# A sink-attention mixer on one core: weight sums by VectorE alone in buffers of their own, made late in two chunks, with the block order of the third batch and the pair order of the last turned

## Chip, cores and metric

The kernel runs on one core of a Trainium2 chip. The metric is device time in microseconds (us); the figure shown is the median of three runs. One further execution was profiled, and all rows below come from it.

## What is computed

```
q, k, v: 4 batches x 8 heads x 768 x 64; n_sink = 4, window = 128
scores = q k^T / 8, kept where column < n_sink or 0 <= row - column < window
x   = softmax(scores) v, heads side by side: 4 x 768 x 512
u   = x + (x^T U V)^T                       U 768 x 32, V 32 x 768
out = u + max(u w_ch1, 0) w_ch2             w_ch1 512 x 2048, w_ch2 2048 x 512
```

## The kernel before

The feed-forward part (FFN) is most of the work. Its 2048 hidden units are 16 **blocks** f of 128; a batch's 768 rows are two **chunks** c of 384. For each batch b, chunk and block, TensorE makes the hidden values (`l1`, L1251 to L1253: 12 matmuls, each number as a high and a low part), ScalarE or VectorE the relu's high part `hh` (L1259, L1260), VectorE its low part `hl` (L1262), and TensorE adds the block's share of the output (`l2`, L1272: 9 matmuls). A block with its weights is one tile `w` of 1 MB. Blocks 0 and 8 stay in two fixed tiles (`w_174`, `w_175`); the other 14 share four tiles (`w_176` to `w_179`) and come back from DRAM copies (`wd`) whenever their turn comes (L522).

Batches are numbered 0 to 3. Batch 0 goes over the blocks in groups while the weights are narrowed to the two-part form on VectorE and ScalarE (L108 to L116, L514). Batches 1 and 2 run one chunk after the other, (1,0), (1,1), (2,0), (2,1), with 16 blocks each: blocks 15 to 0 where c is 0, 0 to 15 where c is 1. So the blocks at a turn are still in their tiles. Beside the FFN of batch b the kernel does the attention of batch b+1 and then its *mixing* (the U V term: L936 to L1030, tiles `xT`, `xhl`, `t`). In the text a block is counted through the kernel: 0 to 31 in batch 0, 32 to 47 in (1,0), 48 to 63 in (1,1), 64 to 79 in (2,0), 80 to 95 in (2,1).

The last batch (`ffn_last`) takes blocks in pairs j = 0 to 7 and makes the hidden values with seven products instead of eight (L1139). For that it needs sums and differences of each pair's weights. `sums` makes them while both blocks lie in their tiles during batches 1 and 2: two adds of high and low part (`w`, 512 wide), four sums or differences 256 wide, then a copy to the high part and a subtraction for the low part, both 1024 wide; 16 stores of 512 KB write them to `sd`. `SUMS` says in which chunk a pair's sums are made: pairs 0 to 3 in (1,1), 7 to 4 in (2,0). The adds go through `tt`, which leaves it to the planner whether VectorE or GpSimd does them; the tiles `a` and `t` come from `raw`, a ring of four buffers `big` that also carries the outputs (L1298) and their residual rows `xd`.

All steps are recorded in a `Plan`. It is run forward and backward over a table of costs, then with shaken priorities from three `SEEDS`; the best order found is written out, engine by engine. Each engine works its list strictly in order, and nearly all DMAs are in one list, SyncE's. 30 idle matmuls fill gaps (L1376).

Of the kernel before, what the change touches and what calls it, by code (L numbers as in the profile page):

```python
# [15 lines left out]
U16 = mybir.dt.uint16  # L16
# [23 lines left out]
NPF = NF // 2  # L40
SUMS = {(1, 1): (0, 1, 2, 3), (2, 0): (7, 6, 5, 4)}
NEG = 8.0e9
# [6 lines left out]
TURNS = 4  # L49
SEEDS = (300012, 300023, 300026,)  # L50
SLACK = 0.0344
# [5 lines left out]
NSTREAM = 4  # L57
NBIG = 4
NNR = 6
NHH = 2  # L60
# [188 lines left out]
class Plan:  # L249
# [116 lines left out]
    def forward(self):  # L366
        avail = dict.fromkeys(self.SYNC, 0.0)
        ready = {e: [] for e in avail}
        dma = port = 0.0

# [33 lines left out]
        while done < len(self.steps):  # L404
# [22 lines left out]
            if e == "SP" and s.lat < 0.0:  # L427
                end = -s.lat
                dma = max(dma, end - 1.3)
            elif e == "SP":  # L430
                dma = max(dma, t + s.dur + 0.65) + s.lat
                end = dma + 1.3
# [47 lines left out]
class Fast:  # L480
# [44 lines left out]
    def narrow(self, src, n, prio, dst=()):  # L525

        raw, A, S_ = self.raw(), self.nr(), self.nr()
        if len(self.early) > 0:
            self.early.pop(0)
            self.plan.add("SP", 0.0, lambda: None, w=(raw,), lat=-EARLY[NBIG - 1 - len(self.early)], prio=-1e6)  # L530
        else:
            self.put(raw, lambda: (raw().bitcast(U16)[:, 1:4 * n + 1], src), P * n * 8, prio - 8.0)
        x = self.bank() if dst else None
        box = {"raw": raw, "a": A, "s": S_}
        cost = (0.069 + n * 0.52e-3, 0.069 + n * 0.26e-3, 0.069 + n * 0.26e-3, dve(n), 0.069 + n * 0.26e-3, dve(n), dve(n))
        steps = narrow_steps(self.nc, raw, n, lambda: A()[:, :n], lambda: S_()[:, :n], x and (lambda: x()[:, :n]))
# [12 lines left out]
        return raw, lambda: f32(raw())[:, 1:2 * n + 1:2]
# [492 lines left out]
    def seven(self, b, t0):  # L1042
# [38 lines left out]
        self.u[b, 0] = out  # L1081

    def sums(self, j, ws, prio):

        a, t = self.raw(), self.raw()
        fa, ft = (lambda x=x: f32(x()[:, :2 * DM]) for x in (a, t))
        for i, w in enumerate(ws):
            self.tt(DM, lambda i=i: fa()[:, i * DM:(i + 1) * DM], lambda w=w: f32(w()[:, 0]), lambda w=w: f32(w()[:, 1]), ALU.add,
                    r=((w, 0), (w, 1)), w=((a, i),), prio=prio)
# [3 lines left out]
        for i, o, x, y, op, r in ((0, s1, a21, a22, ALU.add, []), (1, s2, s1, a11, ALU.subtract, [(t, 0)]),  # L1093
                                  (2, s3, a11, a21, ALU.subtract, []), (3, s4, a12, s2, ALU.subtract, [(t, 1)])):
            self.tt(K2, o, x, y, op, r=[(a, 0), (a, 1)] + r, w=((t, i),), prio=prio)
        hi, lo = (lambda x=x: x()[:, :2 * DM].bitcast(F32R) for x in (a, t))
        self.copy(2 * DM, hi, ft, r=(t,), w=(a,), prio=prio)
        self.tt(2 * DM, lo, ft, lambda: f32(hi()), ALU.subtract, r=(a,), w=(t,), prio=prio)
        sd = self.sd[j]
# [4 lines left out]
    def ffn_last(self, b, prio):  # L1104

        nc, add = self.nc, self.plan.add
        late = self.recent[:]
        order = late[2:] + [None] + late[:2] + [None]
        fixed = [self.w[f] for f in range(NF) if f not in STREAMED]
        slots = [(NRES + self.held[f][0], self.held[f][1], f) if f is not None else (i // 3, fixed[i // 3], None) for i, f in enumerate(order)]  # L1110

# [14 lines left out]
        def l1(n):  # L1126
            j = NPF - 1 - n
            w1, w2, wt = unit(2 * j, self.wd[2 * j]), unit(2 * j + 1, self.wd[2 * j + 1]), unit(None, self.sd[j])
# [51 lines left out]
            p1 = product(x, r12, w1, half(w1, 0), 0, True, self.line)  # L1180
            self.line = (p1,)
            product(y, r2, w1, half(w1, 1), 1, True)
            snap(sa, ta, 0)
# [148 lines left out]
    def run(self):  # L1332
# [7 lines left out]
        self.ust, self.vst = one([P, NB, P], F32R, "ust"), one([P, S], F32R, "vst")  # L1340
        self.t = ring(2, [P, DM], F32R, "t")
        self.wtiles, self.banks, self.bigs, self.accs, tiles = [], [], list(self.early), [], []
        bigs = Ring(NBIG, None)
# [42 lines left out]
        for b in range(B):  # L1386
# [4 lines left out]
            else:  # L1391
# [3 lines left out]
                for c in range(NCHUNK):  # L1395
                    self.ffn(b, c, ORDER[::-1] if c == 0 else ORDER, 70.0 + 80.0 * (NCHUNK * b + c), False)
            if b + 1 < B:
# [165 lines left out]
def sink_attention_mixer(ctx, tc, q, k, v, vs, limits, U, V, w1, w2, out):  # L1563
# [5 lines left out]
    with tc.tile_pool(name="work", bufs=1) as work, tc.tile_pool(name="idle", bufs=1, space=PSUM) as idle, \  # L1569
# [16 lines left out]
        for src, n in ((U, NB * RANK), (V[0], VC), (V[1], VC), (w1[ORDER[0]], DM))[:NBIG]:  # L1586
            early.append(pre.tile([P, RAW], I32, name=f"big{len(early)}"))
            nc.sync.dma_start(early[-1].bitcast(U16)[:, 1:4 * n + 1], src)
        tri = sp.tile([P, 2, P], F32, name="tri")
# [69 lines left out]
```

## Time and profile before

| | |
|---|---|
| median of 3 runs | 747.08 us (745.52 to 747.18) |
| the profiled execution's own time | 747.41 us |
| its span, first to last instruction | 745.7 us |
| TensorE busy | 725.6 us (97%), 4032 matmuls |
| VectorE, ScalarE, GpSimd busy | 494.8, 369.6, 219.8 us |

TensorE's share of 97% counts pipelined matmuls from issue to end. What it waits for is seen better in PEld, its weight loads: one that waits is listed with what it waited for. The granted TensorE clock was full speed in all slices of the page.

### The profile page before, as it was taken

The page shows a single profiled execution, that of the slowest core. Times are in us where ns is not written, and L with a number is a line of the kernel's source. Part 1 is how long each engine was busy: PE and PEld are TensorE (multiplying, and loading weights), DVE is VectorE, ACT ScalarE, POOL GpSimd, SP SyncE. Part 2 cuts the span into 40 slices and gives each one's busy share as a digit, 9 for nine tenths or more (in the row PEclk, how much of TensorE's full clock was granted, in tenths as well). Part 3 has the DMA queues.
Part 4 walks back from the last instruction along what each step waited for, and adds up shares of the span by engine and source line. Part 5 has one row for each costly group of instructions (what it writes and reads, how often), then busy time and mean ns, then how long its engine had stood idle before and what let it go on. Part 6 is the DMA issues. An engine that isn't in the chain of part 4 may idle for free.

```text
span 745.7 us, 11814 instructions
## 1 busy us (share of the span) xinstructions
PE 725.6 (97%) x4032; PEld 626.5 (84%) x4032; DVE 494.8 (66%) x1209; ACT 369.6 (50%) x1029; POOL 219.8 (29%) x337
## 2 busy tenths in 40 slices
PE   8989999999998999999999999999999999999997
PEld 7757877778787999999879998898998989888895
DVE  6899889897899567677975198975667224122233
ACT  5996475775874455555543165654545113121220
POOL 4751040313731153353811055754422000000000
PEclk9999999999999999999999999999999999999999
DMA  7559667765795378663599448984157734366433
GB/s 240 157 181 337 245 238 243 267 239 220 227 288 231 129 218 288 185 211 95 171 332 321 173 141 244 350 278 124 72 183 254 239 129 156 133 236 262 173 113 118
DMA packets 46373, 157.34 MB, mean 211 GB/s; under 512 B 5728, under 2 KB 12512, under 8 KB 36576
## 3 DMA queue, kind: packets, MB, share of 16 engines
q1 hardware_dynamic: 46016, 156.11, 61.7%
q8 instruction: 34, 0.56, 0.3%
q10 hardware_dynamic: 288, 0.39, 0.2%
q14 instruction: 35, 0.29, 0.1%
HBM read 116.37 MB, written 40.11 MB: 210 GB/s over the span
## 4 chain that ended last, share of the span: by engine, by line
PE 78%; DVE 9%; ACT 6%; DMA 4%; issue 2%; POOL 2%; SPq 0%; ACTq 0%; DVEq 0%; POOLq 0%
PE bank L1272 23%; PE bank L1209 9%; PE bank L1251 8%; PE bank L1139 8%; PE bank L1252 8%; PE bank L1253 7%; PE bank L693 2%; PE bank L840 2%; PE bank L791 2%; PE bank L717 2%; ACT p L749 1%; PE bank L737 1%; DMA qkraw<-in_q_dram 1%; PE bank L738 1%; DMA v_raw<-in_v_dram 1%
## 5 line engine op out<-in xcount | busy, mean ns | idle before, releaser
L1272 PE MATMUL bank<-w,hh 128*128 128x512 f32 x576 | 184.1, 401 | 0.0
L1251 PE MATMUL bank<-ul,w 128*128 128x384 f32 x384 | 134.2, 350 | 0.7 <-ACT w L507 0.5
L1252 PE MATMUL bank<-uh,w 128*128 128x384 f32 x384 | 129.3, 337 | 0.4 <-DVE w L514 0.3
L1253 PE MATMUL bank<-uh,w 128*128 128x384 f32 x384 | 129.2, 336 | 0.0
L1272 PEld LDWEIGHTS bank<-w,hh 128*128 128x128 f32 x576 | 103.6, 188 | 17.0 <-issue 2.4
L1272 PE MATMUL bank<-w,hl 128*128 128x512 f32 x288 | 114.2, 396 | 1.9 <-DVE hl L1262 1.9
L1262 DVE SCALAR_TENSOR_TENSOR hl<-bank,hh 128x384 fp32r<-128x384 f32 x96 | 53.0, 552 | 58.7 <-ACT hh L1259 58.0
L1259 ACT ACTIVATE hh<-bank 128x384 fp32r<-128x384 f32 x90 | 44.1, 490 | 92.7 <-PE bank L1253 92.2
L749 ACT ACTIVATE p<-p,ms 128x132 f32<-128x132 f32 (+1 forms) x144 | 70.0, 487 | 33.6 <-DVE ms L746 33.4
L1251 PEld LDWEIGHTS bank<-ul,w 128*128 128x128 f32 x384 | 72.4, 188 | 9.4 <-issue 3.4
L1252 PEld LDWEIGHTS bank<-uh,w 128*128 128x128 f32 x384 | 72.3, 188 | 5.1 <-DVE w L514 1.4
L1253 PEld LDWEIGHTS bank<-uh,w 128*128 128x128 f32 x384 | 72.2, 188 | 0.0
L1272 PEld LDWEIGHTS bank<-w,hl 128*128 128x128 f32 x288 | 54.1, 188 | 15.5 <-DVE hl L1262 3.1
L746 DVE CUSTOM_DVE_ANT_0 p<-bank,mask 128x132 f32<-128x132 f32 (+1 forms) x144 | 54.1, 400 | 14.6 <-PE bank L738 9.7
L516 POOL TENSOR_TENSOR p<-p 128x256 f32<-128x256 f32 (+1 forms) x26 | 21.0, 806 | 76.3 <-ACT p L749 75.2
L1170 DVE TENSOR_TENSOR qkraw<-bank,p 128x384 f32<-128x384 f32 x12 | 6.7, 557 | 54.9 <-PE bank L1139 54.9
L1209 PE MATMUL bank<-w,ul 128*128 128x512 f32 x144 | 39.7, 394 | 0.0
L516 POOL TENSOR_TENSOR ul<-xT,uh 128x384 fp32r<-128x384 f32 x9 | 9.1, 1026 | 83.2 <-ACT uh L507 51.7
L507 ACT COPY p<-bank 128x384 f32<-128x384 f32 x16 | 7.7, 478 | 52.0 <-PE bank L1139 52.0
L1209 PEld LDWEIGHTS bank<-w,ul 128*128 128x128 f32 x144 | 26.9, 187 | 6.0
L817 POOL TENSOR_SCALAR_AFFINE_SELECT oph<-oph 128x384 fp32r<-128x384 f32 (+1 forms) x48 | 28.0, 583 | 5.9 <-ACT oph L507 3.1
L791 PE MATMUL bank<-ident,p 128*128 128x128 f32 x144 | 25.8, 279 | 3.6 <-ACT p L773 2.7
(261 smaller groups left out, 1570.2 us busy)
## 6 DMA issues: line engine op xcount, KB each, us to landing
w<-wd SPq DMA_DIRECT2D x52, 1024.0 KB, 5.4
big<-in_w_dram SPq DMA_DIRECT2D x32, 512.0 KB, 4.5
wd<-w SPq DMA_DIRECT2D x16, 1024.0 KB, 4.6
big<-xd SPq DMA_DIRECT2D x33, 256.0 KB, 3.2
sd<-big SPq DMA_DIRECT2D x16, 512.0 KB, 7.2
w<-sd SPq DMA_DIRECT2D x8, 1024.0 KB, 5.0
qkraw<-in_k_dram SPq DMA_DIRECT2D x32, 198.0 KB, 5.5
qkraw<-in_q_dram SPq DMA_DIRECT2D x32, 192.0 KB, 4.6
```

The costliest lines, as they stand in the source:

```text
L516: ways["POOL"] = (gps(n), lambda: nc.gpsimd.tensor_tensor(dst(), a(), b(), op), True)
L746: add("DVE", dve(wd), lambda: nc.vector.tensor_tensor_reduce(p()[:, u, NS + lo:], st()[:, :wd], self.mask[:, min(qb, 2), lo:], -0.125, 3.0 ...
L749: add("ACT", act(wd) + 0.22, lambda: nc.scalar.activation(p()[:, u, NS + lo:], p()[:, u, NS + lo:], AF.Exp, bias=sm()[:, j:j + 1], scale=-1.0,
L791: nc.tensor.transpose(tr()[:, u * P:(u + 1) * P], p()[:, u, SW + NS:], self.ident)
L1139: nc.tensor.matmul(out(), stat(p, dd), mv(dd), start=first and dd == 0 and k == 0, stop=dd == 1 and k == 2, skip_group_check=True)
L1209: nc.tensor.matmul(accs[k](), a()[:, sl], w()[:, m, :], start=False, stop=n == NPF - 1 and f == 1 and q == 2)
L1251: nc.tensor.matmul(ph()[:, :CH], wh, ul()[:, d, :], start=d == 0, stop=False)
L1252: nc.tensor.matmul(ph()[:, :CH], wl, uh()[:, d, :], start=False, stop=False)
L1253: nc.tensor.matmul(ph()[:, :CH], wh, uh()[:, d, :], start=False, stop=d == NC - 1)
L1259: self.plan.any({"ACT": (act(CH), lambda: nc.scalar.activation(hh(), ph()[:, :CH], AF.Relu)), "DVE": (dve(CH), lambda: nc.vector.tensor_sc ...
L1262: add("DVE", dve(CH), lambda: nc.vector.scalar_tensor_tensor(hl(), ph()[:, :CH], 0.0, f32(hh()), ALU.max, ALU.subtract), r=(ph, hh), w=(hl ...
L1272: nc.tensor.matmul(acc[k](), a()[:, sl], w()[:, m, :], start=not begin and i == 0 and j == 0, stop=i == n - 1 and j == 2)
```

## The change

`sums` makes its adds and subtractions with `vtt`, which offers them to VectorE alone. Its two tiles come from `wsum`, a ring of three buffers of 4 KB per partition that nothing else uses. Copy and subtraction are cut from one of 1024 into four of 256. `SUMS` moves the pairs: 0, 1, 6, 7 in (1,1), and 5, 4, 3, 2 in (2,1). `BACK` turns the third batch (b = 2): (2,0) now runs 0 to 15, and (2,1) 15 to 0. The last batch takes its pairs 0 to 7 instead of 7 to 0 and hands on its tiles accordingly; its second product of a pair is ordered after its first. The seeds are others, and the planner's account of the first loads changes by a line. `NEARLY` equals `NBIG`, so that its two conditions change nothing here.

```
-SUMS = {(1, 1): (0, 1, 2, 3), (2, 0): (7, 6, 5, 4)}
+SUMS = {(1, 1): (0, 1, 6, 7), (2, 1): (5, 4, 3, 2)}
+BACK = ((1, 0), (2, 1))
-SEEDS = (300012, 300023, 300026,)
+SEEDS = (200045, 200056, 200095,)
...
-        dma = port = 0.0
+        port = 0.0
+        dma = max((-s.lat - 1.3 for s in self.steps if s.lat < 0.0), default=0.0)
...
+    def vtt(self, n, dst, a, b, op, **kw):
+        self.plan.any({"DVE": (dve(n), lambda: self.nc.vector.tensor_tensor(dst(), a(), b(), op), True)}, **kw)
...
-        a, t = self.raw(), self.raw()
+        a, t = self.wsum(), self.wsum()
...
-            self.tt(K2, o, x, y, op, r=[(a, 0), (a, 1)] + r, w=((t, i),), prio=prio)
-        self.copy(2 * DM, hi, ft, r=(t,), w=(a,), prio=prio)
-        self.tt(2 * DM, lo, ft, lambda: f32(hi()), ALU.subtract, r=(a,), w=(t,), prio=prio)
+            self.vtt(K2, o, x, y, op, r=[(a, 0), (a, 1)] + r, w=((t, i),), prio=prio)
+        for i in range(4):
+            h, l, x = (lambda i=i, v=v: v()[:, i * K2:(i + 1) * K2] for v in (hi, lo, ft))
+            self.copy(K2, h, x, r=[(t, i)], w=((a, i // 2),), prio=prio)
+            self.vtt(K2, l, x, lambda h=h: f32(h()), ALU.subtract, r=[(a, i // 2)], w=((t, i),), prio=prio)
...
-            j = NPF - 1 - n
+            j = n
...
-            self.line = (p1,)
-            product(y, r2, w1, half(w1, 1), 1, True)
+            self.line = (product(y, r2, w1, half(w1, 1), 1, True, (p1,)),)
...
+        self.wsum = ring(3, [P, 2 * DM], F32R, "wsum")
...
-                    self.ffn(b, c, ORDER[::-1] if c == 0 else ORDER, 70.0 + 80.0 * (NCHUNK * b + c), False)
+                    self.ffn(b, c, ORDER[::-1] if (b, c) in BACK else ORDER, 70.0 + 80.0 * (NCHUNK * b + c), False)
```

The written orders differ on every engine, with the same 7498 TensorE instructions. VectorE has 2965 instructions instead of 2918, ScalarE 1606 instead of 1576, GpSimd 529 instead of 544. SyncE has 514 instead of 510: `w<-wd` is issued 56 times instead of 52. (These counts include the branch for other inputs, which is the same in both and is not run.)

**Place 1, VectorE in the mixing of batch 2's rows (L939 before, L941 now), beside blocks 50 to 52.** `big<-big` and `big<-w` are steps of `sums`. Before:

```order
L1262 SCALAR_TENSOR_TENSOR hl<-bank_166,hh 128x384
L514 TENSOR_TENSOR opl<-bank_170,oph 128x3x128
L514 TENSOR_TENSOR big_109<-big_115 128x256
L514 TENSOR_TENSOR pst<-bank_173,pst 64x384
L514 TENSOR_TENSOR big_109<-big_115,big_109 128x256
L514 TENSOR_TENSOR qs<-qkraw,qs 64x768
L514 TENSOR_TENSOR big_111<-w_178 128x512
L939 TENSOR_TENSOR xT<-xT,bank_170 128x384
L939 TENSOR_TENSOR xT<-xT,bank_173 128x384
L514 TENSOR_TENSOR big_109<-big_109,big_115 128x1024
L939 TENSOR_TENSOR xT<-xT,bank_170 128x384
```

Now:

```order
L941 TENSOR_TENSOR xT<-xT,bank_169 128x384
L516 TENSOR_TENSOR xT<-bank_170,tb 64x384
L941 TENSOR_TENSOR xT<-xT,bank_166 128x384
L510 CAST vhl<-v_raw 128x6x64
L941 TENSOR_TENSOR xT<-xT,bank_170 128x384
L941 TENSOR_TENSOR xT<-xT,bank_166 128x384
L516 TENSOR_TENSOR xT<-bank_169,tb 64x384
L516 TENSOR_TENSOR pst<-bank_168,pst 64x384
L1270 SCALAR_TENSOR_TENSOR hl<-bank_173,hh 128x384
```

The steps of `sums` are gone from between the mixing's adds. The first two pairs' steps now stand earlier, beside the attention at blocks 45 to 50; this is a piece of it, with `hl` of block 45 and 46:

```order
L1087 TENSOR_TENSOR wsum<-w_177 128x512
L1270 SCALAR_TENSOR_TENSOR hl<-bank_167,hh 128x384
L1087 TENSOR_TENSOR wsum<-wsum 128x256
L516 TENSOR_TENSOR opl<-bank_170,oph 128x3x128
L1087 TENSOR_TENSOR wsum<-w_176 128x512
L1087 TENSOR_TENSOR wsum<-wsum 128x256
L1087 TENSOR_TENSOR wsum<-w_179 128x512
L1087 TENSOR_TENSOR wsum<-wsum 128x256 x2
L1270 SCALAR_TENSOR_TENSOR hl<-bank_169,hh 128x384
L1087 TENSOR_TENSOR wsum<-wsum 128x256 x2
```

Pairs 6 and 7 follow beside blocks 58 to 63, where there is no attention, and pairs 5, 4, 3, 2 beside blocks 84 to 93.

**Place 2, SyncE's list at the end of (1,1) and the start of (2,0).** Before:

```order
L522 DMA w_179<-wd_2320 128x2048
L522 DMA w_178<-wd_2533 128x2048
L522 DMA w_177<-wd_2593 128x2048
L522 DMA w_176<-wd_2660 128x2048
L522 DMA out_dram<-big_111 128x512
L522 DMA out_dram<-big_113 128x512
L522 DMA out_dram<-big_115 128x512
L522 DMA qkraw<-in_q_dram 64x768
```

Now:

```order
L524 DMA w_176<-wd_2668 128x2048
L524 DMA sd_4573<-wsum 128x1024
L524 DMA w_179<-wd_902 128x2048
L524 DMA sd_4573<-wsum 128x1024
L524 DMA w_178<-wd_1019 128x2048
L524 DMA sd_4647<-wsum 128x1024
L524 DMA w_177<-wd_1078 128x2048
L524 DMA sd_4647<-wsum 128x1024
L524 DMA w_176<-wd_1250 128x2048
L524 DMA out_dram<-big_111 128x512
```

`wd_2660` and `wd_2668` are block 15's copy, the last of (1,1). Four loads are new, those of blocks 1 to 4 for (2,0), and each stands behind a store of `sd` that waits for `sums`.

**Place 3, VectorE at the end of batch 0, from the low part of block 23 on** (the 24th `hl`); `nr`, `big<-..` and `bank<-..` there are narrowing of weights. Before:

```order
L1262 SCALAR_TENSOR_TENSOR hl<-bank_171,hh 128x384
L116 TENSOR_TENSOR bank_166<-nr,bank_166 128x512
L110 TENSOR_SCALAR nr<-nr 128x512
L111 TENSOR_SCALAR nr<-nr 128x512
L508 CAST xhl<-first1k 128x512
L113 SCALAR_TENSOR_TENSOR nr<-big_115,nr 128x512
L514 TENSOR_TENSOR w_178<-bank_166,w_178 128x512
L114 TENSOR_SCALAR nr<-nr 128x512
L514 TENSOR_TENSOR qs<-qkraw,qs 64x768
```

Now:

```order
L1270 SCALAR_TENSOR_TENSOR hl<-bank_169,hh 128x384
L116 TENSOR_SCALAR nr<-nr 128x512
L516 TENSOR_TENSOR vhl<-v_raw,vhl 128x6x64
L117 SCALAR_TENSOR_TENSOR bank_169<-big_113,nr 128x512
L941 TENSOR_TENSOR xT<-xT,bank_170 128x384
L941 TENSOR_TENSOR xT<-xT,bank_168 128x384
L941 TENSOR_TENSOR xT<-xT,bank_172 128x384
L941 TENSOR_TENSOR xT<-xT,bank_166 128x384
L118 TENSOR_TENSOR bank_169<-nr,bank_169 128x512
```

Four adds of batch 1's mixing, which stood ahead of this `hl`, now stand behind it, and the narrowing comes a step later.

## Rows read from the trace of the kernel before

**Rows 1.** The page: busy time of each engine, its share of the span, and instructions.
```profile
PE 725.6 (97%) x4032; PEld 626.5 (84%) x4032; DVE 494.8 (66%) x1209; ACT 369.6 (50%) x1029; POOL 219.8 (29%) x337
```

**Rows 2.** Busy time by stretch: stretch and its length in us, then PE, PEld, DVE, ACT, POOL busy us (instructions), granted clock, DMA share, GB/s.
```profile
60.00:200.00 140.00, 139.72 (x767) 110.16 (x766) 124.56 (x317) 92.74 (x253) 39.08 (x62) 1.00 0.73 256
200.00:240.00 40.00, 36.23 (x193) 30.47 (x192) 37.66 (x69) 24.63 (x47) 12.92 (x10) 1.00 0.74 249
240.00:340.00 100.00, 100.00 (x583) 91.79 (x582) 66.52 (x174) 51.71 (x163) 37.56 (x69) 1.00 0.62 201
340.00:400.00 60.00, 57.68 (x323) 51.12 (x322) 51.24 (x104) 33.40 (x85) 26.33 (x31) 1.00 0.70 231
440.00:520.00 80.00, 77.72 (x451) 69.01 (x451) 64.92 (x153) 47.24 (x144) 46.27 (x69) 1.00 0.80 253
520.00:612.00 92.00, 92.00 (x501) 83.32 (x500) 46.52 (x105) 33.87 (x87) 20.89 (x30) 1.00 0.50 172
```

**Rows 3.** Waits of TensorE's weight loads (PEld) from 340 to 400 us: who waited for whom, us in total, times, longest.
```profile
PEld bank L936 <- DVE xT L939: 1.1, 2, 0.9
PEld bank L953 <- ACT first1q L507: 1.1, 1, 1.1
PEld bank L791 <- ACT p L773: 1.0, 2, 0.8
PEld bank L976 <- ACT big L507: 0.7, 1, 0.7
PEld bank L1251 <- ACT first1k L507: 0.5, 1, 0.5
```

**Rows 4.** The same from 440 to 520 us.
```profile
PEld bank L791 <- ACT p L773: 3.0, 9, 1.2
PEld bank L840 <- POOL oph L817: 1.7, 2, 1.5
PEld bank L1251 <- DVE ms L746: 0.5, 1, 0.5
```

**Rows 5.** Steps of `sums` in the two stretches, by engine and shape (340 to 400 us first, then 436 to 500 us): count, busy us, mean ns.
```profile
L514 DVE TENSOR_TENSOR big<-big,big 128x1024 fp32r<-128x1024 f32 x3 | 3.9, 1291 | 0.2 <-ACT big L507 0.2
L514 DVE TENSOR_TENSOR big<-w 128x512 f32<-128x512 f32 x4 | 2.9, 734 | 1.3 <-DMA w<-wd 1.2
L514 DVE TENSOR_TENSOR big<-big 128x256 f32<-128x256 f32 x6 | 2.9, 487 | 0.1
L514 DVE TENSOR_TENSOR big<-big,big 128x256 f32<-128x256 f32 x6 | 2.5, 418 | 0.1
L516 POOL TENSOR_TENSOR big<-big,big 128x1024 fp32r<-128x1024 f32 x1 | 2.4, 2402 | 0.0
...
L514 DVE TENSOR_TENSOR big<-big 128x256 f32<-128x256 f32 x6 | 5.0, 829 | 0.1
L514 DVE TENSOR_TENSOR big<-big,big 128x1024 fp32r<-128x1024 f32 x3 | 3.9, 1293 | 0.1
L514 DVE TENSOR_TENSOR big<-w 128x512 f32<-128x512 f32 x4 | 3.2, 799 | 0.0
```

**Rows 6.** The chain of waits from 348 to 377 us, in order of time: start, us, what.
```profile
348.69 5.29 DMA out_dram<-big
354.88 2.95 POOL big L516 x2
375.89 1.06 ACT big L507
377.02 0.47 PE bank L976
```

**Rows 7.** Busy time in the places where sums stand now (columns as in Rows 2).
```profile
324.00:354.00 30.00, 30.00 (x184) 27.77 (x183) 23.21 (x64) 17.46 (x57) 12.15 (x21) 1.00 0.42 131
424.00:432.00 8.00, 8.00 (x42) 7.15 (x41) 3.40 (x6) 2.21 (x5) 1.02 (x1) 1.00 0.00 0
560.00:578.00 18.00, 18.00 (x90) 15.83 (x89) 14.26 (x25) 10.15 (x21) 5.44 (x5) 1.00 0.70 255
```

**Rows 8.** Waits of the weight loads from 200 to 240 us, and the longest of those from 0 to 80 us.
```profile
PEld bank L1272 <- DVE hl L1262: 2.0, 1, 2.0
PEld bank L936 <- DVE xT L939: 1.6, 2, 1.3
PEld bank L1251 <- ACT w L507: 0.9, 1, 0.9
PEld bank L1022 <- DVE t L1004: 0.7, 1, 0.7
...
PEld bank L693 <- POOL qkraw L516: 2.1, 1, 2.1
```

**Rows 9.** Groups of VectorE's instructions over the whole span: count, busy us, mean ns of one, idle before.
```profile
L115 DVE SCALAR_TENSOR_TENSOR bank<-big,nr 128x512 f32<-128x512 uint32 x32 | 22.3, 697 | 0.6
L514 DVE TENSOR_TENSOR qs<-qkraw,qs 64x768 fp32r<-64x768 f32 x14 | 14.2, 1012 | 4.8 <-ACT qs L507 4.5
L939 DVE TENSOR_TENSOR xT<-xT,bank 128x384 f32<-128x384 f32 x24 | 12.3, 549 | 0.4 <-PE bank L936 0.2
L514 DVE TENSOR_TENSOR vhl<-v_raw,vhl 128x384 fp32r<-128x384 f32 x9 | 6.1, 674 | 0.5 <-ACT vhl L507 0.3
```

**Rows 10.** DMA issues: count, KB each, median us to landing.
```profile
w<-wd SPq DMA_DIRECT2D x52, 1024.0 KB, 5.4
```

More of the change, by code (lines that the diff above doesn't have):

```diff
@@ L58 @@
 NBIG = 4
+NEARLY = 4
 NNR = 6
@@ L428, in forward @@
                 end = -s.lat
-                dma = max(dma, end - 1.3)
             elif e == "SP":
@@ L527, in narrow @@
         raw, A, S_ = self.raw(), self.nr(), self.nr()
-        if len(self.early) > 0:
+        if len(self.early) > NBIG - NEARLY:
             self.early.pop(0)
@@ L1081, in seven @@
         self.u[b, 0] = out
+    def vtt(self, n, dst, a, b, op, **kw):
+        self.plan.any({"DVE": (dve(n), lambda: self.nc.vector.tensor_tensor(dst(), a(), b(), op), True)}, **kw)
     def sums(self, j, ws, prio):
-        a, t = self.raw(), self.raw()
-        fa, ft = (lambda x=x: f32(x()[:, :2 * DM]) for x in (a, t))
+        a, t = self.wsum(), self.wsum()
+        fa, ft = (lambda x=x: f32(x()) for x in (a, t))
         for i, w in enumerate(ws):
-            self.tt(DM, lambda i=i: fa()[:, i * DM:(i + 1) * DM], lambda w=w: f32(w()[:, 0]), lambda w=w: f32(w()[:, 1]), ALU.add,
+            self.vtt(DM, lambda i=i: fa()[:, i * DM:(i + 1) * DM], lambda w=w: f32(w()[:, 0]), lambda w=w: f32(w()[:, 1]), ALU.add,
                     r=((w, 0), (w, 1)), w=((a, i),), prio=prio)
@@ L1094, in sums @@
                                   (2, s3, a11, a21, ALU.subtract, []), (3, s4, a12, s2, ALU.subtract, [(t, 1)])):
-            self.tt(K2, o, x, y, op, r=[(a, 0), (a, 1)] + r, w=((t, i),), prio=prio)
-        hi, lo = (lambda x=x: x()[:, :2 * DM].bitcast(F32R) for x in (a, t))
-        self.copy(2 * DM, hi, ft, r=(t,), w=(a,), prio=prio)
-        self.tt(2 * DM, lo, ft, lambda: f32(hi()), ALU.subtract, r=(a,), w=(t,), prio=prio)
+            self.vtt(K2, o, x, y, op, r=[(a, 0), (a, 1)] + r, w=((t, i),), prio=prio)
+        hi, lo = (lambda x=x: x() for x in (a, t))
+        for i in range(4):
+            h, l, x = (lambda i=i, v=v: v()[:, i * K2:(i + 1) * K2] for v in (hi, lo, ft))
+            self.copy(K2, h, x, r=[(t, i)], w=((a, i // 2),), prio=prio)
+            self.vtt(K2, l, x, lambda h=h: f32(h()), ALU.subtract, r=[(a, i // 2)], w=((t, i),), prio=prio)
         sd = self.sd[j]
@@ L1106, in ffn_last @@
         nc, add = self.nc, self.plan.add
[L1107 to L1110, printed above, removed]
+        late = self.recent[::-1]
+        fixed = [f for f in range(NF) if f not in STREAMED]
+        keep = lambda f: (NRES + self.held[f][0], self.held[f][1], f)
+        slots = [(0, self.w[fixed[0]], fixed[0]), keep(late[0]), (1, self.w[fixed[1]], None)]
+        slots += [keep(f) for f in late[1:]]
         def unit(key, dram):
@@ L1587, in sink_attention_mixer @@
             early.append(pre.tile([P, RAW], I32, name=f"big{len(early)}"))
-            nc.sync.dma_start(early[-1].bitcast(U16)[:, 1:4 * n + 1], src)
+            if len(early) <= NEARLY:
+                nc.sync.dma_start(early[-1].bitcast(U16)[:, 1:4 * n + 1], src)
         tri = sp.tile([P, 2, P], F32, name="tri")
```

## The prediction

> **What bounds the kernel now.** I read the page first. TensorE is busy 725.6 of 745.7 us [rows 1]; its matmuls are the same before and after, so only its waits can change. A slower measured time per matmul is not on offer either: the granted clock stands at 1.00 in every stretch of [rows 2], the higher of the two levels.
>
> The next view is busy time by stretch, which tells where the waits are. From 240 to 340 us and from 520 to 612 us TensorE is busy for all of 100.00 and 92.00 us, and from 60 to 200 us for 139.72 of 140 [rows 2]. The losses lie between 340 and 400 us (57.68 of 60), between 440 and 520 us (77.72 of 80) and between 200 and 240 us (36.23 of 40) [rows 2]. The rest is the start and the last store. What separates these stretches from the quiet ones is VectorE: 51.24 of 60 us busy (85%), 64.92 of 80 (81%) and 37.66 of 40 (94%), against 66.52 of 100 and 46.52 of 92 in the quiet ones [rows 2].
>
> The third view is what the weight loads waited for. From 340 to 400 us it is the mixing and the attention, handed over by VectorE and ScalarE: 1.1 + 1.1 + 1.0 + 0.7 + 0.5 = 4.4 us [rows 3]. From 440 to 520 us it is attention, 3.0 + 1.7 + 0.5 = 5.2 us [rows 4]. Together 9.6 us. `sums` itself never stands there, since TensorE does not wait for it; but in just these two stretches its steps sit in VectorE's list between the steps that TensorE does wait for [rows 5]. The chain of waits shows it: from 348 to 377 us it runs through an output's store of 5.29 us, 2.95 us of `sums` on GpSimd that wait for the buffer the store frees, later a copy of `sums` on ScalarE of 1.06 us, and then the late matmul of the mixing at 377.02 [rows 6].
>
> **Part 1: sums out of the two dense stretches.** VectorE has 3.9 + 2.9 + 2.9 + 2.5 = 12.2 us of sums from 340 to 400 us, and 5.0 + 3.9 + 3.2 = 12.1 us in the second stretch [rows 5]. Without them it would be busy 51.24 - 12.2 = 39.0 of 60 us (65%) and 64.92 - 12.1 = 52.8 of 80 us (66%). That is the share of the quiet stretch, 66.52 of 100, which holds attention too and no wait [rows 2]. With the sums gone from there (place 1), the output buffers also stop being shared, so the chain of [rows 6] loses its first links. Bounds of the gain: 0, if attention's own hand-overs were the cause, and 9.6 us. I take 8.0: near the upper end, because the quiet stretches are the nearest rows and show nothing, less about a sixth, since the 3.0 us in nine waits for ScalarE [rows 4] look partly like the attention's own rhythm.
>
> **Part 2: what the sums cost where they are now.** One pair now takes VectorE two adds of 512, four steps and four subtractions of 256. Undisturbed, 512 costs at most 0.73 us and 256 costs 0.42 us [rows 5], so 2 x 0.73 + 8 x 0.42 = 4.8 us, plus the share of the copies that falls to VectorE. Cutting the last subtraction has a price: one of 1024 took 1.29 us, four of 256 take 4 x 0.42 = 1.67 us [rows 5], 0.4 us more per pair, 3 us in all.
>
> [...]
>
> Pairs 0 and 1: beside blocks 45 to 50, which ran from about 324 to 354 us. VectorE was busy there 23.21 of 30 us [rows 7]. Two pairs are 9.6 us, and 23.2 + 9.6 = 32.8 us would not fit into 30. Against this the stretch behind it is emptied (part 1), and in the new order GpSimd takes more of the attention's own steps. It is hidden only as long as the planner keeps attention's steps ahead of them. Bounds: 0, and the 4.4 us that a stretch with a busy VectorE cost [rows 3]. I take 1.5, a third: the total over blocks 44 to 51 stays about as it was, but the margin is gone.
>
> Pairs 6 and 7, at blocks 58 to 63: VectorE has 3.40 of 8 us in such a stretch without attention, and DMA stands at 0.00 [rows 7]. Nothing.
>
> Pairs 5 to 2, at blocks 84 to 93: VectorE is busy 14.26 of 18 us from 560 to 578 us, where it makes the seven operands of the last batch [rows 7]. One pair stands ahead of this stretch, most of another behind it, so that perhaps 3 of the 3.7 free us are used up. What waits is the `hl` of a block; the cover is TensorE's own queue of matmuls. Lower bound 0, upper bound 2.0, the longest single wait for an `hl` [rows 8]; I take 0.5.
>
> **Part 3: the turned batch.** At the seam (1,1) to (2,0) blocks 1 to 4 must be fetched anew (place 2), four loads of 1 MB with 5.4 us from issue to landing each [rows 10]. DMA stood idle from 424 to 432 us [rows 7], and each load has about three blocks of TensorE's work ahead of its use, some 12 us. In return four pairs' stores leave (2,0). Hidden: 0. If the cover goes, each late load costs up to 5.4 us. Between (2,1) and the last batch the tiles still match, so nothing is added there. The second product's fixed order in the last batch changes no amount of work; VectorE has nothing urgent there.
>
> **Part 4: the reordering of everything else.** The orders differ from the first microseconds on, with other seeds. At the start I count no clear difference in the amount of work, but the narrowing of one more half block now stands ahead of the first relus on VectorE. Nearest row: the longest wait of a weight load there, 2.1 us [rows 8], in both directions. I take a loss of 1.0. At the end of batch 0 (place 3) VectorE gets four adds of 549 ns, one `vhl` of 674 and one narrowing step of 697 more between block 23 and block 27, and one `qs` of 1012 less [rows 9]: 2.2 + 0.67 + 0.70 - 1.01 = 2.6 us, where it is already busy at 94% and TensorE waits 2.0 + 1.6 + 0.9 + 0.7 = 5.2 us [rows 8]. Bounds: a loss of 2.6, if every microsecond is passed on, and a gain as large, if the later place of the adds frees the time ahead of them. I take a loss of 1.2.
>
> **The sum.** -8.0 + 1.5 + 0 + 0.5 + 0 + 1.0 + 1.2 = -3.8 us, against the profiled execution's own 747.41 us (1.7 us around its span of 745.7): **743.6 us**. The median of the runs, 747.08, lies 0.3 us lower, too little to matter. A difference under 0.3%, some 2.2 us, is about what a measurement of this kernel can't tell from none.
>
> **Rivals.**
>
> A. *The whole of the waits goes, and the reordering costs nothing.* For it: the quiet stretches. Then 747.4 - 9.6 = 737.8 us, or about 739 with half a microsecond here and there. Against it: the added work at place 3 is in the order.
>
> B. *The gain is spent again.* The 9.6 us were partly attention's own hand-overs (gain 4 to 5), and the early parts and blocks 45 to 50 take it back: -4.5 + 1.5 + 2.1 + 2.6 = +1.7, down to about -1.5 if one of them stays away: 746 to 749 us, no change that can be told. For it: VectorE at 94% at the end of batch 0, and a stretch of 30 us into which 32.8 do not fit. The change would then move the dense place 20 us ahead and not remove it.
>
> C. *Slower: the new loads stand behind the stores.* In SyncE's list each of the four loads for (2,0) waits behind a store of `sd`, which waits for the sums of pairs 6 and 7 (place 2). If those end late, the loads go out late, one after the other. Two of them exposed are 2 x 5.4 = 10.8 us: 743.6 + 10.8 = 754.4 us. It decides from the point at which the sums of pair 7 end more than about 12 us (three blocks) behind their place. Against it: VectorE is less than half busy there [rows 7], so this needs more than one late step.
>
> That the change does not do what it says can be excluded for the adds; of the copies, most still go to ScalarE, as before.
>
> **Chances.** Forecast (a gain of 2.2 to 6 us) 0.46, A 0.14, B 0.23, C or a reordering that costs more than the gain 0.17. So faster by over 0.3% 0.60, within 0.3% 0.23, slower 0.17. The range leaves out the best of A and most of C: 738.8 to 749.6 us; the forecast's own is 741 to 745.
>
> **What would show it.** Part 1: TensorE busy for all but some 1 us of the two stretches of mixing and attention in batches 1 and 2, VectorE near 65% there, and no `wsum` step on the chain of waits in them. Part 2: waits of weight loads of 1 to 2 us at blocks 45 to 52, and `wsum<-wsum` of 256 at about 420 ns. Part 3: no weight load that waits for `w<-wd` at block 65 to 68. Part 4: waits at the end of batch 0 of 6 to 7 us instead of 5.2, and the first block's matmuls about 1 us later. The prediction fails if waits remain in the two stretches although `sums` is gone from them (part 1's cause is wrong), or if more than 4 us appear before 240 us.

## The result, and the profile after

The changed kernel takes **754.39 us** (median of 4 runs, 752.83 to 757.1) against 746.3 us for the kernel before on the same chip: a ratio of 1.0121, with a 95% interval of 1.0096 to 1.0146. It is slower, and outside the range. A second set of runs of it (below) gave 1.0104 (1.0057 to 1.0151). The profiled execution took 755.84 us with a span of 754.1, 8.4 us more than the span before.

First the page's busy times, which answer [rows 1], then the busy times by stretch, which answer [rows 2] (same columns).

```profile
PE 730.7 (97%) x4032; PEld 632.5 (84%) x4032; DVE 494.6 (66%) x1256; ACT 373.2 (49%) x1059; POOL 219.2 (29%) x322
```

```profile
60.00:200.00 140.00, 139.65 (x771) 111.56 (x769) 123.96 (x314) 92.08 (x252) 39.07 (x61) 1.00 0.71 248
200.00:240.00 40.00, 35.08 (x167) 28.37 (x166) 35.33 (x69) 20.63 (x38) 12.13 (x8) 0.91 0.73 238
240.00:340.00 100.00, 99.17 (x574) 90.74 (x573) 66.85 (x174) 54.65 (x173) 46.60 (x65) 1.00 0.65 205
340.00:400.00 60.00, 59.23 (x337) 52.91 (x336) 45.91 (x103) 33.70 (x88) 22.98 (x32) 1.00 0.65 213
440.00:520.00 80.00, 77.20 (x451) 70.68 (x450) 47.94 (x135) 46.11 (x152) 41.31 (x63) 0.98 0.72 231
520.00:612.00 92.00, 89.48 (x486) 81.30 (x485) 63.58 (x150) 37.89 (x99) 21.62 (x32) 0.98 0.62 217
```

TensorE has 5.1 us more of busy time for the same 4032 matmuls. That is the first sign: in [rows 2] the granted clock was 1.00 in every stretch, and now three stretches stand below it. Part of the gain is there too: from 340 to 400 us TensorE is busy for 59.23 us where it was 57.68.

A share of busy time does not tell the clock: from 608 to 611 us TensorE is busy for 2.91 of 3 us at a granted clock of 0.50. So the comparisons below use one more measure. The **lost time** of a stretch is taken from the starts of TensorE's matmuls: from each start to the next, less the lower quartile of that distance for this width in the trace before (0.112 us for 256 columns, 0.173 for 384, 0.231 for 512), added up wherever it exceeds 0.04 us. It holds waits and slow clock alike, and its sum moves with the span. Only its differences are read: 4.9 us of it lie between 240 and 340 us of the kernel before, where no weight load waited and TensorE was busy for all of 100 us.

```
lost time, us     0-60 60-200 200-240 240-340 340-400 400-440 440-560 560-690  sum
before            35.2   25.1     7.6     4.9     7.2     0.3    12.9     0.2  94.3
changed           35.4   24.3    12.3     5.9     5.6     0.5    12.9     6.0 103.7
changed, again    33.8   24.4    11.4     5.7     6.9     0.5    12.1     5.4 102.4
```

(The time to the first start, 0.8 us, has no column here, but it is in the sum, and so are 1.4 us behind 690 us in the last row.) So the change lost 4.7 us at the end of batch 0 and 5.8 us ahead of and in the last batch; from 340 to 400 us it gained 1.6, and from 440 to 560 us, where 12.1 us of sums had gone, nothing.

**At the end of batch 0** the chain of waits of the changed kernel reads (start, us, what):

```profile
212.29 6.16 DMA xd<-first1k
...
221.17 0.54 ACT nr L114
221.73 0.70 DVE nr L115
222.46 1.30 DVE nr L116
223.76 0.61 DVE w L516
224.42 0.45 PE bank L1260
...
231.29 2.87 DVE xT L1032 x6
234.16 0.61 DVE w L516
234.82 3.21 PE bank L1280 x8
```

TensorE waits twice for a narrowed weight `w` (1.5 and 1.7 us at its weight loads): it ends late behind a store's landing and then behind adds into `xT`. Place 3 had shown the narrowing coming a step later. The store itself is not new, since the chain of the kernel before holds it at the same place:

```profile
210.94 6.52 DMA xd<-first1k
```

TensorE's idle time in these 40 us grew only from 3.77 to 4.92 us. Most of the 4.7 us is the clock: at 0.91, by the row above, 40 us withhold some 3.6 us, an estimate: length times (1 - clock).

**At the start of (2,0)**, waits from 445 to 465 us (who waited for whom, us, times, longest; SPq is SyncE's list), and the chain there:

```profile
ACT qs L509 <- issue: 3.9, 1, 3.9
PEld bank L793 <- ACT p L775: 3.6, 3, 3.2
```

```profile
SPq L524 <- DMA out_dram<-big: 5.5, 3, 5.0
```

```profile
455.04 0.83 ACT qs L509
455.87 0.32 ACT p L775
...
456.23 0.92 PE bank L793 x3
```

SyncE stands 5.0 us at a load `big<-xd`, whose buffer is still being stored to the output. Behind it in the list stand the loads of `qkraw`, from which ScalarE makes `qs`.

**Ahead of the last batch**, the chain, and VectorE's wait from 565 to 612 us:

```profile
589.10 9.10 DMA sd<-wsum
598.23 1.30 DVE wsum L1087 x2
599.58 8.47 DMA w<-wd
608.09 0.69 PE bank L1259
608.78 0.32 PE bank L1260
```

```profile
DVE wsum L1087 <- DMA sd<-wsum: 4.9, 4, 1.5
```

A pair takes two of the three buffers. Its second tile must wait until the first store of the pair before has landed; the sums end late, and only then may `w`, which they read, be loaded anew. The matmul behind it takes 0.32 us instead of 0.17. That is the **granted clock**, again by stretch:

```profile
220.00:224.00 4.00, 1.69 (x5) 0.56 (x4) 3.57 (x6) 3.63 (x8) 2.55 (x2) 1.00 0.95 295
224.00:228.00 4.00, 3.58 (x13) 3.40 (x14) 3.70 (x8) 1.71 (x3) 0.00 (x0) 0.66 1.01 384
228.00:234.00 6.00, 5.30 (x20) 3.49 (x18) 5.11 (x11) 1.55 (x3) 2.57 (x2) 0.94 0.07 26
234.00:238.00 4.00, 3.18 (x9) 2.50 (x10) 3.90 (x9) 0.59 (x1) 0.00 (x0) 0.69 0.67 227
...
452.00:456.00 4.00, 1.42 (x7) 0.80 (x5) 0.65 (x3) 0.96 (x2) 0.00 (x0) 1.00 0.98 245
456.00:460.00 4.00, 3.77 (x14) 3.46 (x15) 2.83 (x5) 3.06 (x11) 1.48 (x4) 0.67 0.99 325
...
604.00:608.00 4.00, 1.57 (x7) 0.94 (x5) 1.89 (x6) 0.39 (x1) 0.00 (x0) 0.95 0.99 408
608.00:611.00 3.00, 2.91 (x9) 2.91 (x10) 0.00 (x0) 0.00 (x0) 0.00 (x0) 0.50 0.95 385
```

In the traces of both kernels the clock stands at 1.00 or at 0.50; a row at 0.66 to 0.69 holds some of each (1.00 from 224 to 225 us, 0.50 from 226 to 228). Ahead of three of these falls TensorE had been busy for 1.69, 1.42 and 1.57 us of 4, ahead of the fourth for 5.30 us of 6. Length times (1 - clock) estimates what such a stretch withholds: 1.4, 1.2, 1.3 and 1.5 us in the four rows below 0.70, with the edges left out. With the edges it is about 7 us, an estimate from the rows of the three long stretches above (0.91 of 40, 0.98 of 80, 0.98 of 92). The kernel before shows 1.00 in every stretch of [rows 2], although TensorE was busy there for only 2.48 us of the 4 from 228 us on. At the late load of `w` the order of events is this: TensorE is busy for 0.00 of the 2 us from 606 us on, the clock has a mean of 0.79 from 607 to 608 us, and from 608 to 611 us, where the matmuls go on, it is 0.50.

### The profile page after: what moved, and what is told of

Read it like the earlier page. It is cut to its first block, busy times and chain, and to the rows that moved or that the text cites. A ratio compares the mean times of both kernels' runs of the same rounds, so it can differ in the third digit from the quotient of the medians.

```text
span 754.1 us, 11913 instructions
## 1 busy us (share of the span) xinstructions
PE 730.7 (97%) x4032; PEld 632.5 (84%) x4032; DVE 494.6 (66%) x1256; ACT 373.2 (49%) x1059; POOL 219.2 (29%) x322
## 4 chain that ended last, share of the span: by engine, by line
PE 78%; DMA 8%; DVE 8%; ACT 4%; issue 1%; SPq 0%; ACTq 0%; DVEq 0%
PE bank L1280 23%; PE bank L1217 8%; PE bank L1259 8%; PE bank L1148 8%; PE bank L1261 7%; PE bank L1260 7%; PE bank L842 3%; PE bank L793 2%; PE bank L695 2%; DMA w<-wd 2%; DMA sd<-wsum 2%; DMA qkraw<-in_q_dram 2%; PE bank L739 1%; PE bank L719 1%; PE bank L740 1%
## 5 line engine op out<-in xcount | busy, mean ns | idle before, releaser
L1260 PE MATMUL bank<-uh,w 128*128 128x384 f32 x384 | 130.8, 341 | 1.2 <-DVE w L516 1.2
L1261 PE MATMUL bank<-uh,w 128*128 128x384 f32 x384 | 131.1, 341 | 0.0
L1260 PEld LDWEIGHTS bank<-uh,w 128*128 128x128 f32 x384 | 73.6, 192 | 6.5 <-DVE w L516 1.5
L1261 PEld LDWEIGHTS bank<-uh,w 128*128 128x128 f32 x384 | 73.5, 191 | 0.0
L518 POOL TENSOR_TENSOR p<-p 128x256 f32<-128x256 f32 (+1 forms) x24 | 23.1, 963 | 68.8 <-ACT p L751 68.6
L518 POOL TENSOR_TENSOR ul<-xT,uh 128x384 fp32r<-128x384 f32 x12 | 12.3, 1042 | 91.8 <-DVE ul L516 52.3
L1087 DVE TENSOR_TENSOR wsum<-wsum 128x256 f32<-128x256 f32 (+1 forms) x64 | 28.2, 472 | 5.2 <-DMA sd<-wsum 4.7
```

The lines of the kernel that those rows point to most:

```text
L518: ways["POOL"] = (gps(n), lambda: nc.gpsimd.tensor_tensor(dst(), a(), b(), op), True)
L1260: nc.tensor.matmul(ph()[:, :CH], wl, uh()[:, d, :], start=False, stop=False)
L1261: nc.tensor.matmul(ph()[:, :CH], wh, uh()[:, d, :], start=False, stop=d == NC - 1)
```

## The experiments

Times are medians; the ratio is to the kernel before in the same set of runs. One execution of a kernel can be several us from the next (the kernel before: 741.86 to 749.67 us in one set), and a profile is one of them. So the profile tells where time is lost, and the ratio how much. Each ratio has to be held against the changed kernel's two: 1.0096 to 1.0146 and, in the second set, 1.0057 to 1.0151. The intervals of the first three edits below overlap with one or both of these, so their sizes are not clear of noise one by one.

```
                     us     ratio   95% interval    lost: 200-240 240-340 340-400 440-560 560-690  sum
fourth buffer      752.06  1.0085  1.0059 1.0112        11.4     5.7     5.5    12.7     1.9   97.4
xd later           750.95  1.0054  1.0017 1.0092        11.2     5.9     5.5     9.4     1.9   94.0
early order        753.44  1.0096  1.0067 1.0124         7.9     5.8     5.6    11.8     6.1  100.4
seeds alone        751.20  1.0075  1.0045 1.0105        12.7     5.9     9.4     9.3     0.2   99.4
three together     746.16  1.0009  0.9992 1.0026         7.5     5.8     8.7     8.0     0.7   92.3
sums in (2,0)      751.03  1.0069  1.0049 1.0089         9.1     6.7     6.3    11.3     1.6   97.4
own buffers alone  746.56  1.0018  1.0001 1.0035         5.9     7.0     6.5    11.5     0.1   91.2
old buffers        749.09  1.0044  1.0026 1.0063         8.2     5.8     5.6    12.1     0.9   95.2
no turn            747.25  1.0024  0.9999 1.0049         7.6     7.9     4.7     9.6     3.0   93.5
no turn, four      745.34  0.9996  0.9970 1.0021         5.3     8.2     4.3     9.5     0.8   87.8
other draw         754.67  1.0113  1.0065 1.0161        12.2     7.0     6.9    12.3     5.3  103.7
changed, again     753.82  1.0104  1.0057 1.0151        11.4     5.7     6.9    12.1     5.4  102.4
```

### The fourth buffer

```
-        self.wsum = ring(3, [P, 2 * DM], F32R, "wsum")
+        sums = Ring(3, None)                  # planned as three, so the order stays
+        self.wsum = lambda: sums(lambda i=len(sums.boxes): sumt[i % 4])
```

> The changed kernel with the order of all instructions as it is, and a fourth buffer for the sums (laid over the tiles `nr`, which the preparation of weights has done with by then), so that the second tile of a pair no longer waits for the landing of the store of the pair before. Theory R (the ring of three is what costs): VectorE's four waits for sd<-wsum, 4.9 us in 565 to 612, go, the load of w that TensorE waits for at 608.09 (2.5 us at its matmul, 3.3 at its weight load) is there in time, and the half-clock stretch behind it (about 1.7 us) goes with it: 4 to 5 us, so 749.5 to 750.5 us against 754.4. Theory Q (the transfers of late batch 2 are too many whoever waits): the load of w lands as late as before, 754 to 755 us.

Measured 752.06 us, between the two: 1.6 us above theory R's range and 1.9 below theory Q's. VectorE no longer waits for `sd<-wsum` from 565 to 612 us, the lost time from 560 on falls from 6.0 to 1.9 us, and the clock stays up there:

```profile
600.00:612.00 12.00, 12.00 (x62) 10.74 (x61) 4.36 (x13) 2.21 (x5) 0.00 (x0) 1.00 0.69 269
```

The mechanism is R's; its size in the median is half of what was expected. The load of `w` is not quite in time: the weight load waited 3.3 us for it in the changed kernel, and still 1.9 us here.

```profile
PEld bank L1259 <- DMA w<-wd: 1.9, 2, 1.6
```

### The loads of xd later

```
+LATE, BEHIND = (2635, 2638, 2862), 3177      # big<-xd_1, xd_2, xd_3; a load of q
+        late = [s for s in order if s.n in LATE]
+        order = [s for s in order if s.n not in LATE]
+        at = next(i for i, s in enumerate(order) if s.n == BEHIND) + 1
+        order[at:at] = late
```

> The changed kernel with three issues moved in SyncE's list: the loads big<-xd_1, xd_2 and xd_3 of the end of (1,1) stand ten rows later, behind the loads of the first two pairs of heads of batch 3's attention; nothing reads them for another 80 us. Theory Q (a load that waits for a store of its buffer holds the loads of q and k behind it): SyncE's wait of 5.0 us for out_dram<-big's landing no longer stands ahead of qkraw<-in_q, ScalarE's 3.9 us without work ahead of 455.04 go, TensorE's 2.8 us for ACT p go, and block 68 starts 3 to 4 us earlier: 750.5 to 751.5 us. Rival S (the stretch is short of something else, so that another wait ends last there): under 1 us, 753.5 to 754.5 us.

Measured 750.95 us, within theory Q's range. From 445 to 465 us the weight load's wait for `p` is 0.3 instead of 3.6 us, and TensorE is busy throughout:

```profile
PEld bank L794 <- ACT p L776: 0.3, 2, 0.2
```

```profile
440.00:480.00 40.00, 40.00 (x239) 36.63 (x239) 25.66 (x75) 24.89 (x83) 20.00 (x33) 1.00 0.85 274
```

In the changed kernel TensorE was busy for 37.20 of these 40 us. In this profile the loss behind 595 us is small too, although the list there is the same and VectorE waits for the ring no less than the 4.9 us of the changed kernel:

```profile
DVE wsum L1088 <- DMA sd<-wsum: 5.9, 4, 1.7
```

The load of `w` behind it landed in 6.24 instead of 8.47 us, and from 595 to 625 us 0.6 us were lost instead of 4.3. How much the wait for the ring costs hangs on that landing too. The run's executions lie between 746.8 and 754.0 us, and the profiled one (746.9) is among the fastest, so this part is not put down to the edit.

### The earlier order of the first batch, and the seeds alone

```
-        self.put_back(best[1])
+        self.put_back(list(EARLY_PRIOS) + best[1][len(EARLY_PRIOS):])   # first 1487 steps as before
```

> The changed kernel with the planner's priorities of the kernel before for the first 1487 steps (the first batch and the attention of the second); the order behind them is the changed kernel's to the row. Theory E (the new order of the first batch costs what it lost at blocks 24 to 28): block 24 starts 3.3 us later than in the changed kernel, as in the kernel before, block 28 some 3.2 us earlier, and the end 3 us earlier: 751 to 752 us. Rival (the loss at blocks 24 to 28 comes with the load on the memory or with the clock, not with the order): 754 to 755 us.

Measured 753.44 us, between the two ranges. In the stretch theory E holds: 7.9 us lost from 200 to 240 us as before the change (7.6), and a granted clock of 1.00. But the first 200 us had been better in the changed kernel, and 1.8 us of that are given back: block 24 starts 5.3 us later than in the changed kernel and not 3.3, block 28 only 1.6 us earlier and not 3.2. So the median says little by itself. Nor are the priorities the kernel before's order to the row: TensorE's order leaves it at 10 us already.

```
-SEEDS = (300012, 300023, 300026,)
+SEEDS = (200045, 200056, 200095,)
```

> The kernel before with the three new seeds alone: same sums, same block order, same tiles, another order drawn by the planner. Theory E2 (what the order lost at blocks 24 to 28 is the draw's): block 24 some 3 us earlier, block 28 some 3 us later than in the kernel before, and the end within 2 us of 749.5. Rival N (the draw is worth nothing by itself; the sums and the turned batch bring the loss): 746 to 747 us. A result above 751 would say that the draw alone is as large as the whole loss.

Measured 751.20 us: the kernel before with nothing but another draw is 5.3 us slower, most of it in the same stretch and for the same `w` (TensorE's weight loads, 200 to 240 us):

```profile
PEld bank L1251 <- ACT w L507: 3.2, 2, 2.3
PEld bank L1252 <- DVE w L514: 2.1, 2, 1.5
```

So this loss needs neither sums nor turn. It goes with the order of the first batch.

### All three edits together

> The changed kernel with all three edits so far: the fourth buffer, the three xd loads ten rows later, and the earlier priorities for the first 1487 steps. Each took something off the changed kernel by itself (754.4 to 752.1, 751.0 and 753.4). Theory Add (three separate losses, at 200 to 240, at 440 to 480 and at 595 to 625): TensorE's lost time there falls to about 8, 2.5 and under 1 us, and the time to 743 to 746 us, at or below the kernel before (745.9). Rival Same (the fourth buffer and the later loads took the same loss, and another wait ends last behind them): 748 to 750 us.

Measured 746.16 us, ratio 1.0009, 0.2 us above theory Add's range and far below rival Same's. Its interval lies below both of the changed kernel's. The three places are separate, and with them the whole loss against the kernel before goes. What kept it from more is a fourth place. Up to 380 us its TensorE order is that of the run with the earlier order alone; there one store landed in 4.41 us, here in 5.99 (chains, then 370 to 390 us, that run first each time):

```profile
374.68 4.41 DMA xd<-first1q
```

```profile
373.70 5.99 DMA xd<-first1q
```

```profile
370.00:390.00 20.00, 19.43 (x112) 17.23 (x111) 10.64 (x20) 9.56 (x18) 2.31 (x2) 1.00 0.86 288
```

```profile
370.00:390.00 20.00, 17.87 (x95) 15.75 (x94) 9.18 (x17) 9.16 (x17) 2.31 (x2) 0.91 0.74 235
```

1.6 us more of landing became 3.1 us of lost time (5.6 and 8.7 from 340 to 400 us), and behind the longer wait the clock fell. This is one execution of each.

### Parts of the change alone

Places back, with the turn:

```
-SUMS = {(1, 1): (0, 1, 6, 7), (2, 1): (5, 4, 3, 2)}
+SUMS = {(1, 1): (0, 1, 2, 3), (2, 0): (4, 5, 6, 7)}
```

> The changed kernel with the earlier priorities, and the places of the sums turned back: pairs 0 to 3 in (1,1) and pairs 4 to 7 in (2,0), still on VectorE, in buffers of their own, with the turned third batch. Theory P (the loss at 595 to 625 is that of sums in (2,1), whose stores and reads of w hold the last loads of w): that loss, 5.2 us in the run with the earlier order, goes to under 1 us, and the stretches 340 to 560 take 1 to 3 us more: 749 to 751 us against 753.4. Rival T (the turned order itself, by its four loads of w at the end of the third batch, brings the loss): it stays at 3 to 6 us, 754 to 757 us.

751.03 us, the upper end of theory P's range; TensorE waits for no `w<-wd` from 590 to 625 us. The loss from 560 us on is 1.6 us and not under 1, and the stretches from 340 to 560 us took 0.2 us more where theory P had 1 to 3.

The kernel before with `vtt`, the cut copies and `wsum` (the diff's new `sums`), nothing else:

> The kernel before with one part of the change: the sums on VectorE alone, in chunks, in three buffers of their own; places, block order, seeds and the order of the first batch as before. Theory G (the gain that was forecast is that of taking the sums out of the stretches of attention, which this edit does not do): 745 to 748 us, no gain. Rival O (buffers of their own free the raw tiles, and that is the gain): 341 to 400 loses 2 us less than the 7.2 of before, 742 to 744 us. Rival R (three buffers hold VectorE by the landing of stores): over 748 us, with waits of VectorE for sd<-wsum of some 5 us.

746.56 us, ratio 1.0018: theory G. Buffers of their own are no gain (340 to 400 us loses 6.5 instead of 7.2).

The changed kernel, with the earlier order, and `sums` as it was before:

> The changed kernel with the earlier priorities and one part undone: the sums take raw tiles, on VectorE or GpSimd, in whole widths, as in the kernel before; places and turned order as changed. Theory P (place and turn bring the losses at 440 to 480 and 595 to 625): both stay, 752 to 755 us against 753.4. Rival R (the three buffers bring the loss at 595 to 625): it falls to under 1 us, 748 to 750 us.

749.09 us, theory R: 0.9 us lost behind 560 us. This run gives back GpSimd and the whole widths too; that it is the ring is shown by the fourth buffer, which changed nothing else. In the profiles 2.0 to 5.4 us are lost from 595 to 625 us in five of the six executions with late places and a ring of three (0.6 in the sixth, the run with `xd` later), and at most 0.7 us in each of the others. So the loss there needs both.

The kernel before with the new `sums` at late places, but no turn:

```
-SUMS = {(1, 1): (0, 1, 2, 3), (2, 0): (7, 6, 5, 4)}
+SUMS = {(1, 1): (0, 1, 6, 7), (2, 1): (2, 3, 4, 5)}
```

> The kernel before with the sums on VectorE in three buffers of their own and at late places (pairs 0, 1, 6, 7 in (1,1), pairs 2 to 5 in (2,1)), but without the turn: old block order of the third batch, old order of the last batch's pairs, no further loads of w, old seeds and old order of the first batch. Theory G (taking the sums out of the dense stretches is the gain, and the turn spends it): TensorE loses 2 to 4 us less than before from 340 to 560 (20.1 us in the kernel before) and nothing new behind it, 742 to 744.5 us against 745.9. Rival L (late places bring the loss at 595 to 625 with any block order, since the stores and reads of w by sums then hold the last loads): 4 to 7 us appear between 560 and 660, 747 to 751 us. Rival N (the stretches' waits are the attention's own): 745 to 747 us.

747.25 us, which is rival L's range, but G's gain and L's loss are both in it. The ratio can't be told from 1. In the two stretches TensorE is busy for more of the time than before:

```profile
340.00:400.00 60.00, 59.75 (x341) 53.88 (x340) 46.20 (x105) 32.39 (x85) 20.26 (x25) 1.00 0.66 219
440.00:520.00 80.00, 79.18 (x465) 71.86 (x464) 53.25 (x139) 42.68 (x141) 38.04 (x61) 1.00 0.62 195
```

From 340 to 560 us 14.3 us are lost instead of 20.1, 5.8 less. Not all of that is the places: the run with own buffers alone, which differs from this one in `SUMS` only, loses 18.0 us there, so that moving the sums is worth 3.7 of it. The gain is spent at two places: 3.0 us more from 240 to 340 us, where weight loads now wait for ScalarE's `p` (first row), nearly all of it ahead of 325 us and so ahead of these sums, which begin at 334 us, and 2.8 from 560 us on behind the ring of three (VectorE's wait from 565 to 612 us, second).

```profile
PEld bank L793 <- ACT p L775: 3.5, 9, 1.0
```

```profile
DVE wsum L1087 <- DMA sd<-wsum: 4.9, 2, 2.5
```

The same kernel with the fourth buffer, in the same order:

> The kernel without the turn (sums late, on VectorE, in buffers of their own), in the same order, with the fourth buffer for the sums over the tiles `nr`. Theory R (its loss of 2.8 us from 560 to 625 is VectorE's wait for the landing of sd<-wsum, 4.9 us there, which holds the last loads of w): the wait and the loss go, and the time is 742.5 to 745 us, 0.996 to 0.999 of the kernel before. Rival Q (the loads are late because of what else is moved there): the loss stays over 2 us, 746 to 748 us.

745.34 us, ratio 0.9996 (0.9970 to 1.0021). VectorE's wait is gone and the loss from 560 us is 0.8. The time lies just above theory R's range, 1.9 us below the kernel with three buffers, though the two intervals overlap. It has the lowest ratio here and can't be told from the kernel before. Its profiled execution, 741.53 us, is one of its fastest.

Two pairs of runs differ by the turn and what comes with it (the order of the pairs and of their second product, the seeds, the planner's account of the first loads): ratios of 1.0018 against 1.0069 with the sums early (own buffers alone, sums in (2,0)), and of 1.0024 against 1.0096 with them late (no turn, early order). The intervals of a pair don't overlap, while moving the sums alone changes neither kernel clearly. But in the profiles the first pair's spans differ by 7.1 us, of which 4.8 are there when block 24 starts, and the second's by 7.5, of which 4.6: in batch 0, ahead of anything that turns. No run has the turn alone, or the planner's new line alone, so what each of them costs is not shown.

### The changed kernel with the old seeds, and once more

> The changed kernel with the seeds of the kernel before: all of the change but for them. Theory D (the draw of the order by itself moves a kernel by 3 to 6 us, as it moved the kernel before by 5.6): at least one of the losses at 200 to 240, 440 to 480 and 595 to 625 is under 1 us above the kernel before, and the time 747 to 752 us. Rival C (the losses belong to the change, whatever the draw): all three stay, 753 to 756 us.

754.67 us: theory D fails on the time, which is rival C's. From 440 to 560 us less is lost than in the kernel before (12.3 against 12.9), but 12.2 us from 200 to 240 and 5.3 from 560 on stay. The old seeds do not bring back the old order, since the planner draws from other inputs now.

> The changed kernel once more, beside these runs on the same chip. Expected 753 to 755.5 us, 1.009 to 1.014 of the kernel before, with the three losses in the same places. If one of them is missing in this execution, it hangs on when a transfer lands and not on the order alone.

753.82 us, with the losses in the same three places: the wait for the narrowed `w`, ScalarE's late `p`, and the load of `w` ahead of the last batch. A fourth came in this execution: the 1.4 us behind 690 us.

## Why the prediction was wrong

- **Part 1 (-8.0): too large, its cause only a part, and little of it arrived.** Without the turn the two stretches lose 5.8 us less, of which moving the sums is 3.7 by the run with own buffers alone, against the -8.0 + 1.5 that parts 1 and 2 gave them. In the changed kernel it is 1.6, all of it from 340 to 400 us. VectorE came to 60% of the second stretch (47.94 of 80), below the 66% forecast; what waited there was a load in SyncE's list. In the first it came to 77% (45.91 of 60), because 8.95 us of sums still run behind 340 us. The step that failed is that a stretch with VectorE at 65% has no waits: TensorE waited 2.8 us for `p` in the stretch with 60%. The prediction's own sign of failure is met: waits remain although `sums` is gone. One reading was off as well: the prediction says that `sums` never stands among the waits of TensorE, but the 0.7 us for `ACT big` in [rows 3] is the very copy that it names in [rows 6].
- **Part 2: pairs 5 to 2 (+0.5)** are the largest miss: 5.8 us. I asked whether VectorE had time for `hl`, and not who waits for `w` while the sums read it, nor what a third buffer waits for. A piece of 256 has a median of 418 ns, as in [rows 5]. **Pairs 0 and 1 (+1.5)** cost little where I put it. Blocks 45 to 50 ran from 334 to 370 us, and the weight loads waited 1.2 us in all there. VectorE was busy for 28.47 us of the first 30, and TensorE had work throughout, so here a busy VectorE alone made no wait:

```profile
333.00:363.00 30.00, 30.00 (x178) 27.31 (x177) 28.47 (x72) 19.62 (x63) 17.09 (x26) 1.00 0.48 149
```

- **Part 3 ("Hidden: 0")**: the four new loads were hidden, and no weight load at blocks 65 to 68 waits for one. What the prediction left out is what stands behind them in the list: the stores, the `xd` loads that wait for a store to land, and q and k of the attention behind those. Moving three loads gave 3.5 us there (12.9 to 9.4). "Nothing is added" between (2,1) and the last batch was wrong as well, for part 2's reason.
- **Part 4**: the start (+1.0) was nothing clear (+0.2 and -1.4 in two executions). The end of batch 0 (+1.2, bounds of 2.6 either way) was +4.7 and +3.8. The place was right; the bounds were not. TensorE's idle time there grew by 1.15 us, much as forecast, with 7.8 us of waits of weight loads (6 to 7 were expected). The rest is the half clock behind the waits, some 3.6 us, for which the sum had no term.
- **No term for the clock.** From "1.00 in every stretch" I concluded that it was not on offer. As a loss it came behind waits of TensorE: the four half-clock stretches of the changed trace from 200 to 620 us withhold 5.4 us by the rows above, about 7 with their edges, against the 8.4 us by which the span grew. [rows 2] begin at 60 us, and the page shows the clock in tenths; ahead of that the kernel before had 0.94 (the changed one 0.97):

```profile
0.00:60.00 60.00, 53.91 (x384) 40.33 (x385) 49.73 (x189) 47.71 (x167) 32.01 (x63) 0.94 0.60 193
```

- **Rival C** named 754.4 us, which is where the time fell, and SyncE's list as the place. But its price was another: two late loads of 5.4 us each at the seam. These were not late, so its figure was met by chance.

What stays open: why the old order of batch 0's end is better cannot be put down to one step, since every draw moves many. The turn and the planner's new line have no run of their own. Whether two landings of the same store differ by other traffic or by chance was not tried.

## What to carry to other kernels

Price a moved transfer by everything queued behind it, and by the buffer that it keeps until it lands: here a load nobody needed for 80 us held up an attention, and a ring one buffer short held a weight tile. Ask of each wait of TensorE whether a half-clock stretch may follow it; four did here from 200 to 620 us, at 1.2 to 1.5 us each, and behind the wait of 1.4 us for `w` from 664 to 668 us of the changed kernel the clock stayed at 1.00. And where a planner draws the order anew, run the old kernel with a new draw first: 5.3 us of difference came from that alone.

## What the runs showed of the hardware

The same store, behind the same order of TensorE, landed in 4.41 and in 5.99 us in two kernels, and only behind the longer one did the granted clock fall (0.91 as a mean of 370 to 390 us against 1.00). Executions of one kernel differed by up to 8.7 us (741.15 to 749.8 us for the kernel without the turn and with four buffers). Behind much the same wait of VectorE for a buffer (4.9 and 5.9 us), a load of `w` that landed in 8.47 us went with 4.3 us of lost time, and one that landed in 6.24 us with 0.6.
